# Top-32 attention with two feed-forward blocks on one core: mask into SBUF, short v matmuls, fixed scale for p, new instruction order

## The chip, the cores and the metric

The kernel runs on one core of a Trainium2 chip. The metric is the device time of one execution in microseconds, the median of several runs. One run more was recorded by the hardware profiler, and its trace is what the rows below come from.

## What is computed

```python
def _attn_ref(q, k, v):                       # (4, 8, 576, 64) each, float32
    scores = scale * np.matmul(q, k.transpose(0, 1, 3, 2))
    kth = np.partition(scores, -top_k, axis=-1)[..., -top_k:-top_k + 1]   # top_k = 32
    scores = np.where(scores >= kth, scores, -1000000000.0)
    attn = np.exp(scores - np.max(scores, axis=-1, keepdims=True))
    attn = attn / (np.sum(attn, axis=-1, keepdims=True) + 1e-09)
    return np.matmul(attn, v)
def _moe_ref(x, w_in, w_out):                 # x (2304, 512), w_in (512, 2048)
    h = x @ w_in
    return (h * (1.0 / (1.0 + np.exp(-1.702 * h)))) @ w_out
def _moe2_ref(x, w1, w2, w3, w_out):          # w1, w2 (512, 1024), w3 (1024, 1024)
    return (((x @ w1) * (x @ w2)) @ w3) @ w_out
```

The heads' outputs are put side by side as a (2304, 512) matrix, which goes through the first block and then through the second. The weights come as 64-bit floats.

## The kernel before, in words

**Tiles.** The 2304 rows are 18 tiles of 128. Each tile needs 8 heads of attention, so there are 144 heads, counted here from 0 (head 24 is the first of tile 3). Products are made in float16 with every operand split into a high and a low half: a block costs three matmuls, high by high, high by low and low by high (`product_op`, L780 to L782). A tile takes 168 such matmuls of 512 columns.

**A head** (`head`). Scores go into one of two PSUM score banks `s_ps` (L1084). VectorE takes the 32 largest by four maxima (L1106) and three replacements (L1109). ScalarE then masks in the bank itself (`f_cut`, L1124) and takes the exponential from the bank into SBUF (`f_exp`, L1127), after which the bank is free. The result is split into halves (L1133 or L1186, then L1136 and L1139), turned by a DMA transpose, and multiplied by v (`f_av`, L1154). For each head that is nine matmuls: five with the high half of the weights by 129 columns (64 of v's low half, 64 of its high half and one of ones), four with the low half by 65. ScalarE or VectorE copies the high part out (`f_x0`, L1209), and VectorE adds the low part (`f_x1`, L1213).

**A tile's blocks** (`moe`). Each operand is scaled by a row's mean of absolute values before it is split: x2 by L1360 and a reciprocal (L1377), p by one more ScalarE pass per half (`f_pa`, L1432), two VectorE steps (`f_psc`, L1438 and L1439) and the scaled split of `split_op` (L417, L420, L427, L430 to L440).

**Weights** (`weights`). 72 blocks of 512 KB are loaded, joined to 32-bit floats (L514), scaled by a norm (`l2_scale`) and split; w3's blocks are turned by four float32 matmuls with a scaled identity (`split_turned`, L677) and multiplied into w_out once (192 of the 512-column matmuls).

**Order.** All operations are recorded by `Order.op` and issued in the order of the table `PLAN`, which holds for each a rank and which of its alternatives (engine and form) is used. Each engine runs its own instructions strictly in that order, SP's DMA queue too.

Of the kernel before, what the change touches and what calls it, by code (L numbers as in the profile page):

```python
# [11 lines left out]
F32 = mybir.dt.float32  # L12
# [9 lines left out]
P = 128  # L22
# [15 lines left out]
class Order:  # L38
    GAP = {"T": 0.25, "V": 0.16, "A": 0.16, "G": 0.1, "D": 0.05, "N": 0.0}
    SAME = {"T": 0.0, "V": 0.11, "A": 0.12, "G": 0.1, "D": 0.25, "N": 0.0}  # L40
    DMA = 2.1
    COLD = ((100.0, 1.3), (300.0, 1.04))
# [33 lines left out]
    def run(self, log=None):  # L76
        free = dict.fromkeys("TVAGD", 0.0)
        lock = moved = 0.0
        for o in sorted(self.ops, key=lambda o: o.rank):
# [26 lines left out]
            if e == "D":  # L106
                moved = max(moved, now) + o.data
                o.end = max(o.end, moved) + o.lat
# [33 lines left out]
    'c-jq@1w$6i0)@9`Hl}uV_O;`sL_k8q4iH2@P(-l1yE{I+ySux)ySux)yIb%556?NzIkKcnNWv1AJW@U>zZB>#D1~@~y^3T=RAQ1X3CWfGq}<*--YBWKH'  # L142
    '%2NZX;L=HUkZ>4c*{$*rEyZYH^Lh!B}&z$no@gjGjBVoqf|?3BF&fLrA(=*)Kco;?du)t9pP;q+s!*jS}yIBc1gRvpS)jVE5v>Dnm*0s7Scp%x->&t=D'
    'jH0jOB6by_>wpq*u~=>4&8H`1ll(!(@NClYCb8lWWS`<sI@apCU>z-vPc;l*<Z`a(VN5qoop(D&_Fz^m?U2k|aUN^g2>@$ww;XEiILik|bX#)*I(7Csm'
    'RxDM%{pEh?3iLZvis6>n9khD4+=sfbioN|q9&dfw(zXKA!lL24^?m3m2IrOHxosgHM(G)<}~{pTI--5_n021v7{rP2ZEuryFwB5m>RmySsDq=V84?@8&'
    '5G*{Xu9rvD<&Pm&)``&*NkaNfvB*TZv+2s84UCHC)l>_9$@(t;?R8S6)qvZ!ul23|HhTK5DC;9pW%0Y6BoJTG#mzCq?Dl(N5<(59}<nD5clqzLNSyDBr'
    'j#OW2AT^X4NsXmeQX8p<)K6ODo#Q>^-5h&a+A6)4`b!HMENpP9LHF2^(hzBaG%R*z?2g!@v7MyF(n@KS)J2*sO_8Qbr(<7wUwHp`*GlW8OVSnTs&q}dF'
    '5QxDOAn>T(i7>a^h`P}Ka!uwPvvLwOZk=jS^gsbk^jp7WL=@k2kE<4mNhxMoJ;;D{gt5X_=L+*a#5cIxst5QIel`=!E$Z6sT?PllPk;VK5gW_@+hA%@>'
    'scv+)?f=_mc<7!{zdFnp{V&E033F$xGzrK5Kjy%B$qf@;09{@?&|0yjDIeACaHSFXW%Hq*zLJC5IBEgennAS*4&7tb{0~l?0`c(q8GN^igUmEtC#QSEa'
    'WyP${Y;DV3C3$`ECmvR>Jt>{L1`J(Y3FWM!GMO_`+3Q06L&l!MAe<&*MD`J*gU)+w8nW6DkCv9et`qMTE%DzBAqimXD_R7=S9d|LRlmfOn_az&r2J~ia'  # L150
    'Va;n_c=Rdi>JX+3@JNpclC&*Lfl5#D%gFIcHD-V=c%j<nM$UEiwa!;R;K6B)GavyoJ&tiF{yip!1uk+dKb4<P<&ye@~T$QiM59OKiQTe2NMZPH?l&|}|'
    '@p&hIl@G{o<?lYSVk!&dOFp;c*D_R&%fDpi>ngdG_i}!vu<uM|qoOLB0u+BGKq;h@P|7RSm9|RVa%&njX>_B}QRPaxC*|Ih8>*~rw4~9dM(xV2Xw;?A%'
    '0_3E3(7;~k@8mgs(e>|E4qqRTP>t|)v_vA^Q$@4a5bA6uLi5hYOeS&HApS4{#6v!Qkm+iIn+F=kLs^Rt08JBzbL;%zesh4T0&i;MyP3OIW<GA7T;B^uJ'
# [111 lines left out]
def kernel(  # L265
# [274 lines left out]
    def l2_scale(Es, turned=None, free=(), inv=None):  # L540
# [47 lines left out]
        if turned is None:  # L588
            return inv, sc, c
# [942 lines left out]
```

## Time and profile before

| what | value |
|---|---|
| median of three runs | 1005.24 us (1004.66 to 1005.38) |
| span of the profiled execution, first to last instruction | 1003.2 us |
| PE busy | 942.3 us, 94% |
| DVE busy | 916.6 us, 91% |
| ACT busy | 803.6 us, 80% |
| POOL busy | 811.5 us, 81% |

The profiled execution is told by its span; what lies around it makes the runs some 2 us longer. PE is TensorE's matmuls, DVE VectorE, ACT ScalarE, POOL GpSimd, SP the engine whose queue issues the DMAs. A busy time is the union of an engine's records, and records of consecutive instructions overlap: the pace of an engine is the distance from one start to the next.

### The profile page before, as it was taken

What the parts mean: (1) busy time and instruction counts of PE and PEld (TensorE: products, weight loads), DVE (VectorE), ACT (ScalarE), POOL (GpSimd) and SP (SyncE); (2) the same over time, 40 slices, a digit from 0 to 9 for tenths busy, and PEclk for the clock granted to TensorE, in tenths of its full rate; (3) what the DMA queues carried; (4) which work ended last, traced back from release to release, by engine and by line L of the source; (5) the groups of instructions that cost most, each with busy time, mean ns of one, the idle gap of its engine ahead of it and who ended that gap; (6) DMA issues with size and microseconds to landing.
All of it is one profiled execution on the core that took longest, in us unless ns stands there. A gap on an engine that the chain in (4) does not pass through costs nothing. (4 is left out here: it accounts for less than half of the span.)

```text
span 1003.2 us, 18918 instructions
## 1 busy us (share of the span) xinstructions
PE 942.3 (94%) x6011; PEld 497.7 (50%) x6011; DVE 916.6 (91%) x2012; ACT 803.6 (80%) x1519; POOL 811.5 (81%) x1199
## 2 busy tenths in 40 slices
PE   5688987899999989999999999999999999999998
PEld 3345553444545444555555555555455555554553
DVE  4899999999999999999999999999999999999543
ACT  7998999987878877998888987888797786756442
POOL 5977889988898999899989988989896886857212
PEclk7799998999999999999999999999999999999999
DMA  9999877977687676888777777767865967644301
GB/s 318 274 291 281 248 187 166 207 142 123 110 141 137 141 135 118 161 142 153 142 158 142 136 139 134 141 118 156 147 123 97 169 122 124 117 95 96 58 11 53
DMA packets 398564, 149.28 MB, mean 149 GB/s; under 512 B 376576, under 2 KB 384768, under 8 KB 398464
## 3 DMA queue, kind: packets, MB, share of 16 engines
q1 hardware_dynamic: 398464, 148.07, 71.9%
q8 instruction: 47, 0.77, 0.3%
q14 instruction: 53, 0.43, 0.2%
HBM read 52.43 MB, written 4.72 MB: 57 GB/s over the span
## 5 line engine op out<-in xcount | busy, mean ns | idle before, releaser
L1106 DVE MAX8 m8s<-ysb 128x8 f32<-128x576 f32 x432 | 322.6, 754 | 5.1
L1109 DVE MATCH_REPLACE8 ysb<-m8s,ysb 128x576 f32<-128x576 f32 x288 | 214.0, 743 | 0.0
L1139 POOL TENSOR_TENSOR ysb<-ysb 128x512 f16<-128x512 f32 x143 | 165.3, 1159 | 2.9 <-ACT ysb L1133 2.2
L1124 ACT ACTIVATE s_ps<-s_ps,m8s 128x576 f32<-128x576 f32 x144 | 102.4, 711 | 53.7 <-DVE m8s L1106 52.9
L780 PE MATMUL mm<-w,usb 128*128 128x512 f16 x350 | 133.1, 380 | 1.5 <-DMA usb<-usb 1.5
L782 PE MATMUL mm<-w,usb 128*128 128x512 f16 x350 | 132.9, 380 | 0.0
L781 PE MATMUL mm<-w,usb 128*128 128x512 f16 x350 | 132.9, 380 | 0.0
L782 PEld LDWEIGHTS <-usb 128*128 128x128 f16 x828 | 81.1, 98 | 98.6 <-issue 1.3
L1127 ACT ACTIVATE ysb<-s_ps,nbs,asm 128x576 f32<-128x576 f32 x144 | 119.7, 831 | 10.7 <-POOL nbs L1116 2.9
L780 PEld LDWEIGHTS <-usb 128*128 128x128 f16 x828 | 81.1, 98 | 90.3 <-issue 5.3
L781 PEld LDWEIGHTS <-usb 128*128 128x128 f16 x828 | 81.2, 98 | 83.9 <-issue 3.9
L1106 DVE MAX8 m8s<-s_ps 128x8 f32<-128x576 f32 x144 | 108.9, 756 | 9.8 <-PE s_ps L1084 7.7
L1084 PE MATMUL s_ps<-kts,qts 128*128 128x288 f16 (+1 forms) x640 | 96.9, 290 | 14.4 <-ACT ysb L1127 13.2
L780 PE MATMUL mm<-wout,usb 128*128 128x512 f16 x279 | 106.3, 381 | 2.2 <-DVE win L514 1.3
L1109 DVE MATCH_REPLACE8 ysb<-m8s,s_ps 128x576 f32<-128x576 f32 x144 | 107.7, 748 | 0.0
L782 PE MATMUL mm<-wout,usb 128*128 128x512 f16 x279 | 106.2, 381 | 0.0
L781 PE MATMUL mm<-wout,usb 128*128 128x512 f16 x279 | 106.2, 381 | 0.0
L1084 PEld LDWEIGHTS <-qts 128*128 128x128 f16 (+1 forms) x640 | 56.1, 101 | 59.5 <-issue 30.1
L1320 POOL TENSOR_TENSOR usb<-usb 128x512 f32<-128x512 f32 x57 | 72.4, 1272 | 12.4 <-issue 7.9
L1154 PEld LDWEIGHTS <-ats 128*128 128x128 f16 (+1 forms) x1440 | 73.8, 101 | 15.5 <-issue 4.2
L1154 PE MATMUL mm<-v2s,ats 128*128 128x129 f16 (+3 forms) x1440 | 77.2, 210 | 0.5 <-DMA ats<-ysb 0.3
L780 PE MATMUL mm<-win,usb 128*128 128x512 f16 x199 | 75.8, 381 | 0.4 <-DMA usb<-tsb 0.4
(374 smaller groups left out, 2235.8 us busy)
## 6 DMA issues: line engine op xcount, KB each, us to landing
w<-in_moe_w_out_dram SPq DMA_DIRECT2D x24, 512.0 KB, 5.5
w<-in_moe_w_dram SPq DMA_DIRECT2D x22, 512.0 KB, 5.8
w<-in_moe_w_in_dram SPq DMA_DIRECT2D x16, 512.0 KB, 5.6
qts<-qts SPq DMA_DIRECT2D x34, 128.0 KB, 2.4
out_dram<-usb SPq DMA_DIRECT2D x17, 256.0 KB, 2.4
usb<-in_q_dram SPq DMA_DIRECT2D x15, 256.0 KB, 3.5
usb<-in_k_dram SPq DMA_DIRECT2D x12, 256.0 KB, 3.0
usb<-in_v_dram SPq DMA_DIRECT2D x11, 256.0 KB, 3.1
```

Of the source, the lines that this page charges most:

```text
L780: nc.tensor.matmul(o, a[:, i, :], hi, start=(first and i == 0), stop=False)
L781: nc.tensor.matmul(o, a[:, i, :], lo, start=False, stop=False)
L782: nc.tensor.matmul(o, a[:, 4 + i, :], hi, start=False, stop=(last and i == 3))
L1084: nc.tensor.matmul(E["sp"][r : r + n, i], qe[q_][:, h, r : r + n], kt[:, j, i * HS : (i + 1) * HS], start=k_ == 0, stop=k_ == 1,)
L1106: nc.vector.max(out=E["m8"][:, 8 * i : 8 * i + 8], in_=E["sp"] if i == 0 else E["w"])
L1109: nc.vector.match_replace(out=two(E["w"]) if i == 0 else E["w"], in_to_replace=E["m8"][:, 8 * i : 8 * i + 8], in_values=E["sp"] if i == 0 ...
L1124: nc.scalar.activation(E["sp"], E["sp"], AF.Prelu, bias=E["m8"][:, TOPK - 1 : TOPK], scale=-1.0, alpha=1.0 / FAR)
L1127: nc.scalar.activation(two(E["y"]), E["sp"], AF.Exp, bias=E["nb"], scale=nesc)
L1139: return lambda: eng.tensor_tensor(hl()[:, S + SR : 2 * S], E["y"][:, 0:SM], hl()[:, 0:SM], op=ALU.subtract)
L1154: nc.tensor.matmul(heads_av()[r : r + n, j_, c0 : P + 1], e["at"][:, i, r : r + n], v2[:, j_, blk, c0 : P + 1], start=(i == 0), stop=(i == 8),
L1320: nc.gpsimd.tensor_tensor(E["f"], E["f"], E["f2"], op=ALU.mult)
```

## The change

What it does:

- The mask writes to an SBUF buffer of the pool `y`, and the exponential works in place there; the score bank is given back after the mask.
- In `f_av` all nine matmuls of a head take 65 columns (v's high half and the ones), and the five of the high half are each followed by one of 64 columns with v's low half into the same columns; each loads its weights anew. `f_x1` is gone.
- p is no longer measured: its scale is one constant, worked out once from the weights' norms (`q12`, `f_pinv`); p is split by `hi_lo`, without a scale.
- x2's scale comes from a sum of squares and the exponent bits of that sum, two small VectorE steps in place of a reciprocal.
- A w3 block may be turned by four transposes instead of four matmuls; the scale is then applied in the two copies.
- The scale factors of scores take two POOL steps instead of three; k's norm carries the 1/8.
- `PLAN` is new for all operations, and the planner's costs differ a little.

```diff
-    COLD = ((100.0, 1.3), (300.0, 1.04))
+    COLD = ((50.0, 1.28), (100.0, 1.03))
...
 PLAN = (
...
     def split_turned(W, scaled, E):
...
+        def f_in_t():
+            E["by"] = by
+            for i in range(4):
+                nc.tensor.transpose(bank()[:, i], W["w"][:, i * P : (i + 1) * P], ident)
...
+        def f_lo_t():
+            nc.vector.scalar_tensor_tensor(E["t"][:, 4:8], bank(), by, E["t"][:, 0:4], op0=ALU.mult, op1=ALU.subtract)
...
+        def f_both():
+            nc.vector.tensor_tensor(q12[:, 0:2], q12[:, 0:2], q12[:, 2:4], op=ALU.mult)
+
+        def f_across():
+            nc.tensor.matmul(M["mm"][0:2, 0:P], q12[:, 0:2], ident, start=True, stop=True)
+
+        def f_most():
+            nc.vector.tensor_reduce(most[0:2], M["mm"][0:2, 0:P], axis=mybir.AxisListType.X, op=ALU.max)
+
+        def f_all():
+            nc.tensor.matmul(M["mm"][:, 0:1], ones[0:2], upper(most)[0:2], start=True, stop=True)
...
-                    nc.gpsimd.tensor_scalar(e, kv_, sm[i, 1:2], D ** -0.5, op0=ALU.mult, op1=ALU.mult)
-
-                    nc.gpsimd.tensor_scalar(e, e, 2.0 ** -40, 2.0 ** 44, op0=ALU.max, op1=ALU.min)
-                    nc.gpsimd.tensor_scalar(sm[i, 8 + h0 : 8 + h1], e, -FAR, 1.0, op0=ALU.mult, op1=ALU.mult)
+                    nc.gpsimd.tensor_scalar(e, kv_, sm[i, 1:2], 2.0 ** 44, op0=ALU.mult, op1=ALU.min)
+                    nc.gpsimd.tensor_scalar(sm[i, 8 + h0 : 8 + h1], e, -FAR, -FAR * 2.0 ** -48, op0=ALU.mult, op1=ALU.add)
...
-            nc.scalar.activation(E["sp"], E["sp"], AF.Prelu, bias=E["m8"][:, TOPK - 1 : TOPK], scale=-1.0, alpha=1.0 / FAR)
+            nc.scalar.activation(two(E["y"]), E["sp"], AF.Prelu, bias=E["m8"][:, TOPK - 1 : TOPK], scale=-1.0, alpha=1.0 / FAR)
 
         def f_exp():
-            nc.scalar.activation(two(E["y"]), E["sp"], AF.Exp, bias=E["nb"], scale=nesc)
+            nc.scalar.activation(E["y"], E["y"], AF.Exp, bias=E["nb"], scale=nesc)
...
-                        c0 = 0 if i < 5 else D
+                        at_ = e["at"][:, i, r : r + n]
                         nc.tensor.matmul(
-                            heads_av()[r : r + n, j_, c0 : P + 1], e["at"][:, i, r : r + n], v2[:, j_, blk, c0 : P + 1],
-                            start=(i == 0), stop=(i == 8),
+                            heads_av()[r : r + n, j_, 0 : D + 1], at_, v2[:, j_, blk, D : P + 1], start=(i == 0), stop=(i == 8),
                         )
+                        if i < 5:
+                            nc.tensor.matmul(heads_av()[r : r + n, j_, 0:D], at_, v2[:, j_, blk, 0:D], start=False, stop=False)
...
-            def f_x1():
-                xs = X["x"][:, 2 * hp : 2 * hp + 2, 0:D]
-                nc.vector.tensor_tensor(xs, xs, heads_av()[:, :, 0:D], op=ALU.add)
...
-            nc.scalar.activation(x2e["h"][:, 0:C], x2e["mm"], AF.Abs, bias=tiny, scale=G13, accum_out=inv2)
+            nc.scalar.activation(x2e["h"][:, 0:C].bitcast(BF16), x2e["mm"], AF.Square, scale=2.0 ** 20, accum_out=inv2)
...
-            def f_pa(Ea=Ea, j=j):
-                nc.scalar.activation(Ea["f"], Ea["p"], AF.Abs, scale=G13, accum_out=pacc[j])
...
-            lo = split_op(
-                due, lambda E=E: E["h"][:, 0:C], lambda E=E: E["h"][:, C : 2 * C], lambda E=E: E["p"], psc, C, [c], E, ["p"],
-                acq=["h"], tag="p ", lo_dve=W,
-            )
+            lo = hi_lo(due, E, lambda E=E: E["p"], [pd[j]], ["p"], tag="p ")
```

What the new table makes of the order is shown at three places. The first is on PE, in the middle of one head's product with v: `ats` is the turned attention, `v2s` holds v's halves and `mm` is a PSUM bank. Before, from the last matmul of the high half on:

```order
L1154 LDWEIGHTS ats
L1154 MATMUL mm_96<-v2s,ats 128x129
L1154 LDWEIGHTS ats
L1154 MATMUL mm_96<-v2s,ats 128x65
L1154 LDWEIGHTS ats
```

And now, from the first matmul of a head on:

```order
L1195 LDWEIGHTS ats
L1195 MATMUL mm_96<-v2s,ats 128x65
L1199 LDWEIGHTS ats
L1199 MATMUL mm_96<-v2s,ats 128x64
L1195 LDWEIGHTS ats
```

Five wide matmuls of a head have become five pairs of short ones, with twice the weight loads; the four short ones behind them stay.

The second place is on DVE, the last rows ahead of the first maximum of head 24 (the last row in each fence). `ysb` and `s_ps` hold scores, `m8s` maxima, `wsm` constants of the weights, `xsb` the attention's output. Before:

```order
L1109 MATCH_REPLACE ysb<-m8s,ysb 128x576
L1213 TENSOR_TENSOR xsb<-xsb,mm_96 128x2x64
L888 RECIPROCAL wsm<-wsm 128x1
L1106 MAX m8s<-ysb 128x8
L889 RECIPROCAL wsm<-wsm 128x1
L1109 MATCH_REPLACE ysb<-m8s,ysb 128x576
L1106 MAX m8s<-s_ps_93 128x8
```

Now:

```order
L1150 MATCH_REPLACE ysb<-m8s,s_ps_94 128x576
L892 TENSOR_TENSOR wsm<-wsm 128x2
L1147 MAX m8s<-ysb 128x8
L893 TENSOR_TENSOR wsm<-wsm 128x1
L1150 MATCH_REPLACE ysb<-m8s,ysb 128x576
L1147 MAX m8s<-s_ps_93 128x8
```

The addition L1213 has gone, and the small steps on the weights' constants, which are more than before, stand further back.

The third place is on ACT, at the mask of head 60. Before, mask and exponential:

```order
L1124 ACTIVATE s_ps_93<-s_ps_93,m8s 128x2x288
L1127 ACTIVATE ysb<-s_ps_93,nbs,asm 128x576
L1028 ACTIVATE usb,asm<-usb,nbs 128x512
L1133 CAST ysb<-ysb 128x576
L965 COPY kvinv<-mm_96 128x1
```

Now:

```order
L1165 ACTIVATE ysb<-s_ps_93,m8s 128x576
L1168 ACTIVATE ysb<-ysb,nbs,asm 128x576
L1313 CAST usb<-usb 128x512
L1168 ACTIVATE ysb<-ysb,nbs,asm 128x576
L1174 CAST ysb<-ysb 128x576
```

The mask is the only one of the two that reads the score bank now, so exponentials stand where their other inputs allow and hold no bank.

## Rows read from the trace of the kernel before

**Rows 1.** Stretches: length, busy us (instructions) by engine, PE clock share, DMA share, GB/s.
```profile
0.00:50.00 50.00, 28.51 (x167) 17.49 (x168) 33.30 (x82) 43.05 (x91) 35.93 (x65) 0.76 0.98 296
50.00:125.00 75.00, 64.10 (x400) 38.37 (x399) 72.32 (x148) 68.43 (x122) 59.36 (x92) 0.98 0.97 275
125.00:200.00 75.00, 62.60 (x458) 35.10 (x456) 72.92 (x175) 73.51 (x141) 70.26 (x104) 0.93 0.84 184
200.00:237.50 37.50, 35.01 (x200) 17.74 (x201) 37.02 (x89) 33.59 (x61) 31.92 (x50) 1.00 0.73 138
237.50:400.00 162.50, 154.74 (x1037) 80.15 (x1035) 157.02 (x347) 129.91 (x251) 145.25 (x224) 0.99 0.71 131
400.00:925.00 525.00, 523.58 (x3314) 271.87 (x3312) 507.84 (x1111) 428.23 (x808) 449.45 (x643) 1.00 0.73 134
925.00:1003.20 78.20, 73.72 (x444) 36.95 (x442) 36.16 (x66) 26.87 (x53) 19.35 (x27) 0.99 0.19 42
```
**Rows 2.** The stretch from head 24's first maximum to the end, same columns.
```profile
237.50:1003.20 765.70, 752.03 (x4791) 388.97 (x4788) 701.01 (x1522) 585.00 (x1110) 614.05 (x892) 1.00 0.67 124
```
**Rows 3.** DVE in order of time: start us, us, instruction.
```profile
237.51 0.76 DVE L1106 MAX8 m8s<-s_ps 128x8 f32<-128x576 f32 x1
...
604.29 0.28 DVE L1213 TENSOR_TENSOR xsb<-xsb,mm 128x128 f32<-128x128 f32 x1
604.49 0.75 DVE L1106 MAX8 m8s<-ysb 128x8 f32<-128x576 f32 x1
...
611.27 0.16 DVE L963 RECIPROCAL kvc<-mm 128x1 f32<-128x1 f32 x1
611.35 0.74 DVE L1106 MAX8 m8s<-ysb 128x8 f32<-128x576 f32 x1
...
992.09 0.69 DVE L729 CAST tsb<-mm 128x512 f16<-128x512 f32 x1 [0.44 <-PE mm L711]
992.70 0.74 DVE L427 SCALAR_TENSOR_TENSOR usb<-psb,msm,usb 128x512 f16<-128x512 f32 x1
```
**Rows 4.** Who waited for whom from 225 to 400 us: total us, times, longest.
```profile
PE s_ps L1084 <- ACT ysb L1127: 6.8, 7, 2.9
```
**Rows 5.** PE in order of time around one pair of heads' product with v.
```profile
608.56 0.98 PE L1154 MATMUL mm<-v2s,ats 128*128 128x129 f16 x18
609.38 0.17 PE L953 MATMUL mm<-kvc,ones 128*128 128x1 bf16 x1
```
**Rows 6.** The chain that ended last: one 512-column matmul; 8 of 128 columns.
```profile
788.36 0.22 PE mm L781
...
947.66 0.45 PE mm L711 x8
```
**Rows 7.** PE in order of time among the weights: float32 and 16-bit matmuls.
```profile
75.42 1.05 PE L677 MATMUL mm<-tsb,win 128*128 128x128 f32 x8
76.52 1.05 PE L677 MATMUL mm<-tsb,win 128*128 128x128 f32 x8
...
137.27 1.10 PE L611 MATMUL mm<-w,tsb 128*128 128x512 f32 x2
138.21 0.38 PE L612 MATMUL mm<-wout,ident 128*128 128x512 f16 x1
```
**Rows 8.** Groups by line and shape: busy us, mean ns of one, idle before.
```profile
L1127 ACT ACTIVATE ysb<-s_ps,nbs,asm 128x576 f32<-128x576 f32 x144 | 119.7, 831 | 10.7 <-POOL nbs L1116 2.9 <-DVE nbs L1116 2.0 <-ACT usb L1311 0.5
L1124 ACT ACTIVATE s_ps<-s_ps,m8s 128x576 f32<-128x576 f32 x144 | 102.4, 711 | 53.7 <-DVE m8s L1106 52.9
L1432 ACT ACTIVATE usb<-psb 128x512 f32<-128x512 f32 x34 | 21.2, 626 | 14.5 <-POOL psb L1418 8.8 <-DVE psb L1412 5.7
L417 ACT ACTIVATE usb<-psb,msm 128x512 f16<-128x512 f32 x21 | 14.7, 714 | 1.1 <-DVE msm L1439 1.1
L1282 POOL TENSOR_TENSOR usb<-usb 128x512 f16<-128x512 f32 x57 | 65.9, 1158 | 2.1 <-ACT usb L1276 1.8
L430 POOL TENSOR_SCALAR psb<-psb,msm 128x512 f32<-128x512 f32 x12 | 8.3, 690 | 1.0 <-ACT usb L417 0.9
```

More of the change, by code (lines that the diff above doesn't have):

```diff
@@ L106, in run @@
             if e == "D":
-                moved = max(moved, now) + o.data
+                moved = max(moved, now + 0.3) + o.data
                 o.end = max(o.end, moved) + o.lat
@@ L545, in l2_scale @@
         sc = wcol()
-        d, ss = sc, inv
+        d, ss = sc if cols is None else cols, inv
         prev = None
@@ L866, in weights @@
         c_in, rin, r12 = wcols(NG), wcols(NG), wcols(2)
-        imax, c_x2, c_out, top, top3 = wcol(), wcol(), wcol(), wcol(), wcol()
+        imax, c_x2, c_out, top, top3, most, pinv = wcol(), wcol(), wcol(), wcol(), wcol(), wcol(), wcol()
         g13 = [(g[0], g[2]) for g in g3]
@@ L897, in weights @@
         ready["c12"] = dve_chain(
-            0.0, f_12, deps=d12 + [d4, ready["rin"]] + [g[1] for g in g13] + ready["in12"], rel=[("f", {"z": tsb[:, 0, :]}, "z")], tag="c"
+            0.0, f_12, deps=d12 + [pmost, d4, ready["rin"]] + [g[1] for g in g13] + ready["in12"], rel=[("f", {"z": tsb[:, 0, :]}, "z")], tag="c"
         )
@@ L957, in kv_prep @@
             2.1 if is_v else 1.7, due - 6, f_load, env=E, acq=[stage, "rest"] + (["v2"] if is_v else ["h", "kr", "kt"]), tag="kv load",
-            data=1.2, after=last_of.get(("load", is_v)),
+            lat=3.05, data=0.55, after=last_of.get(("load", is_v)),
         )
@@ L962, in kv_prep, with f_inv, f_inv_v @@
         s = pe(0.15, due - 1000, f_sum, deps=[a], env=E, acq=[("mm", E, "sum")], tag="kv sum")
-        c = dve(0.12, due, lambda: nc.vector.reciprocal(sc, E["sum"][:, 0:1]), deps=[s], tag="kv scale")
+        c = dve(0.085, due, lambda: nc.vector.reciprocal(sc, E["sum"][:, 0:1]), deps=[s], tag="kv scale")
+        part = 1.0 if is_v else D ** -0.5
+        def f_inv():
+            nc.scalar.activation(inv, E["sum"][:, 0:1], AF.Copy, scale=part)
+        def f_inv_v():
+            nc.vector.tensor_scalar(inv, E["sum"][:, 0:1], part, None, op0=ALU.mult)
         kinv = op(
-            [("A", 0.2, lambda: nc.scalar.copy(inv, E["sum"][:, 0:1]), 0.0), ("V", 0.12, lambda: nc.vector.tensor_copy(inv, E["sum"][:, 0:1]), 0.0)],
+            [("A", 0.05, f_inv, 0.0), ("V", 0.065, f_inv_v, 0.0)],
             due, deps=[c], env=E, rel=[("mm", E, "sum")], tag="kv inv",
@@ L1293, in moe @@
         xinv = mo[:, 0:1]
[L1294 to L1297 removed]
+        inv2, sc2, sg, uo = [mo[:, 2 + i : 3 + i] for i in range(4)]
+        thsc = mo[:, 6:10]
+        ths = pool(0.23, due - 30, lambda: nc.gpsimd.tensor_scalar(thsc, c_in, xinv, 1.0, op0=ALU.mult, op1=ALU.mult), deps=xt + [ready["c_in"]], tag="thsc")
         gs = []
@@ L1368, in f_lo, with f_sc2 @@
             )
+        def f_sc2():
+            nc.vector.tensor_scalar(
+                sc2.bitcast(U32), inv2.bitcast(U32), -1.0, float(223 << 23), op0=ALU.mult, op1=ALU.add
+            )
         def f_t2():
```

388 lines of the change are left out of this document (198 added, 190 removed).

## The prediction

> **What bounds the kernel now.** I read the stretches first, because shares over the whole span hide that the bound changes hands. From 50 to 237.5 us DVE is busy for 182.3 of 187.5 us and PE for 161.7 [rows 1]: VectorE sets the pace. From 125 to 200 us two others are as full: ACT 73.5 and POOL 70.3 of 75 us. From 400 to 925 us PE is busy for 523.6 of 525 us: TensorE sets the pace, and a faster VectorE is worth nothing there. Between 237.5 and 400 us both are near the top (154.7 and 157.0 of 162.5). The first 50 us belong to neither: PE has 28.5 us at a granted clock of 0.76, a mixture of its two levels 1.2 and 2.4 GHz, and the DMA engines are full at 0.98.
>
> So I cut the span where the bound changes hands, at head 24's first maximum on DVE, at 237.51 us [rows 3]. Behind it PE has 752.0 us of work in 765.7 us [rows 2]; 13.7 us are idle. PE's last matmuls end at about 999.2 us, so some 4 us of the idle time are the copy and the store of the last output. Of the rest the largest part has one cause: from 225 to 400 us PE waited seven times, 6.8 us in all, with a score product for the exponential that still read the bank [rows 4].
>
> The time after is then: when head 24 is reached, by VectorE's queue; what PE has left to do behind it; and what is left of PE's idle time.
>
> **VectorE's queue ahead of head 24.** Counted in the built order, ahead of that maximum, by start-to-start distances:
> - ten additions `f_x1` are gone, 0.20 us each (604.29 to 604.49) [rows 3]: -2.0 us;
> - five 512-wide scalings out of a bank and two casts fewer, mostly w3's blocks, priced as the cast, 0.61 us (992.09 to 992.70) [rows 3]: -4.3 us. The seven transposed w3 blocks add a 512-wide step each, but ten other steps of a weight split have gone, so the count of those stays level;
> - two 256-wide split steps fewer, about 0.4 us each, being half a 512-wide one and a fixed part: -0.8 us;
> - six small steps more (the scale from squares, the constant for p), one wider copy more, 0.08 us each for the small (611.27 to 611.35) [rows 3]: +0.8 us.
> The sum is -6.3 us. Some 18 us go over the whole kernel, for there are 72 additions, but what lies behind head 24 buys little while PE is full.
>
> **PE's queue.** The 3216 matmuls of 512 columns stay, at 0.22 us [rows 6], but 330 of them now stand ahead of head 24 where 342 did: twelve, 2.6 us, move behind it. Among the weights seven w3 blocks lose four float32 matmuls (1.10 us a block) and one 16-bit matmul (0.22), and gain four transposes. No row shows such a transpose; between four 128-column 16-bit matmuls (0.23 us) and the four it replaces (1.10) I take 0.35, the near end, as a transpose multiplies nothing. Against that seven more splits use a float32 pass of 0.94 us plus 0.22 [rows 7], and ten simple ones of 0.22 have gone. In all 7 x (0.35 - 1.32) + 7 x 1.16 - 2.2 = -0.9 us, ahead of head 24, where PE is not the bound: I count nothing.
>
> The product with v changes form. A pair of heads takes 18 matmuls in 0.82 us (608.56 to 609.38) [rows 5]; eight 128-column matmuls take 0.45, 0.056 each [rows 6]. Ten of 129 columns are then 0.57, and the eight short ones have 0.25 left, 0.032 each; if they cost by columns alone, 0.0285. I take 0.030. Now 28 x 0.030 = 0.84, against the 0.82 of before. Over 80 such groups (72 pairs, eight of which are cut at a batch's end and issue everything twice) that is +1.6 us, between -1.7 (at 0.0285) and +5.3 (at 0.032) without rounding, and +1.3 of it behind head 24. PE's work behind head 24 grows by 2.6 + 1.3 = 3.9 us.
>
> Here a rule speaks against the change. The trace shows a weight load ahead of every matmul and 128-column pairs at 0.056 us each [rows 6]. The Trainium skill (TensorE: Matmul & The Clock Gate, section Back-to-back issue gap) says that in a real stream of LDWEIGHTS and MATMUL pairs at N=128 about 81 ns pass per matmul. By it a pair of heads would take 2.27 us and the kernel some 116 us more; the trace does not agree (56 ns), so the sum goes by the rows.
>
> **PE's idle time.** The bank is now given back by the mask, and the exponential (0.83 us [rows 8]) and whatever stands between the two hold it no longer. Seven waits averaged 0.97 us, one of 2.9 us [rows 4]; each gets shorter by at least the 0.83 us. I count -4 us; the ends are 0, if PE's next matmuls wait for something else, and -6.8 us.
>
> **What costs nothing, and under what cover.** ACT loses 36 passes `f_pa` of 0.63 us and some 77 scaled passes of 0.71, and gains 31 casts [rows 8], at most 0.71: some 55 us fewer of 803.6. The mask now goes from PSUM to SBUF and the exponential from SBUF to SBUF. No row has these forms with these functions; the bounds are the two old durations, 0.71 and 0.83 [rows 8], so the pair costs up to 0.12 us more or less per head, 17 us at most, under what ACT loses. The Trainium skill (ScalarE: Activation LUTs, section Step-by-step) holds that ScalarE writes PSUM faster than SBUF, which would make the mask dearer; it changes no sum here, as ACT is busy for 585.0 of 765.7 us from 237.5 us on [rows 2], but it counts from 125 to 200 us, in a rival below.
> POOL gains ten 512-wide subtractions (1.16) and 49 scalings (0.69 [rows 8]), 45 us at most, and loses some 60 small steps: of its 40 idle us ahead of head 24, 4.7 lie between 125 and 200 us [rows 1], but most of the new work stands earlier. SP's queue has the same number of DMAs, and the 64th of 72 weight loads stands behind the 11th transpose of attention in both orders.
> p's split no longer waits for both halves of p, and loses about 1 us of latency; PE has other tiles' work over it, up to the end: nothing.
>
> **The sum.** -6.3 + 3.9 - 4.0 = -6.4 us on the span of 1003.2, so 996.8 us. The median of the runs is 2.0 us above that span: **998.8 us**.
>
> **The rivals.**
> *The pace was never VectorE's alone* (same). ACT and POOL are as full as DVE from 125 to 200 us. If they gate head 24, the -6.3 does not come, +3.9 is matched by idle time that PE had there, and the shorter waits for a score bank give back a microsecond or two: 1004 us. For it: 73.5 of 75 us on ACT. Against: ACT has less to do, POOL room before 125 us.
> *Short matmuls are held by their weight loads* (slower). Place: the 28 in a row of every pair, where now at most four stand in a row; the four may live on a load made early under a wide matmul. Price: 2240 of them. The gain of 6.4 us is gone when each takes 0.033 instead of 0.030, and at 0.038, nearer to the group's present mean of 0.046, they add 18 us: 1017 us. For it: nothing shows a long row. Against: the eight left-over short ones came out at 0.032 although each second to fourth had only a short one to hide under.
> *The skill's 81 ns* is the far end of the same mechanism: 1113 us, one chance in a hundred, since the 56 ns contradict it.
> *Constants arrive late* (slower). The chain of small VectorE steps that ends in `r12`, for which the first scaled copy of a waits (L1400, before at 254 us), now has five further links and is finished two heads later, behind head 28 instead of 26. If PE has nothing else ready, it stands for some of these two heads, 5 us or more in all: 1004 to 1009 us. Against: the order puts other tiles' products there.
> *The start gets shorter as well* (faster). Only 5.9 us of VectorE work stands ahead of the first maximum, by the same prices, where 11.3 did, and 16.7 of DVE's first 50 us are idle [rows 1]. If heads start 5 us earlier and keep that, 994; with all of the score waits gone too, 988 us.
>
> **How the numbers follow.** Two runs of this kernel differ by up to 0.7 us, so 0.2%, 2 us, is about what can be told from no change. The forecast's case has 0.52 (991 to 1002), the shorter start 0.14, no change 0.14, the two slower ones 0.11 and 0.08, the rule's 0.01. Faster by over 0.2%: 0.66; within: 0.14; slower: 0.20. The range that leaves out the lowest of the short starts and the dear half of the short matmuls is 986 to 1010.
>
> **What would show it.** Right: head 24's first maximum near 231 us; no wait of a score product for an exponential behind 225 us; a pair's 28 matmuls within 0.81 to 0.90 us; PE full from about 390 us. Wrong: 28 matmuls in over 0.95 us; head 24 at 237 us with ACT or POOL without gaps before it; PE idle around 250 to 265 us while the first copy of a waits for `wsm`.

## The result and the profile after

The changed kernel takes 992.06 us (median of four runs, 990.51 to 994.35) against 1004.95 us for the kernel before (1004.41 to 1005.38): a ratio of 0.9872, 95% interval 0.9853 to 0.9891, or 12.9 us less. A second set of runs on another chip gave 990.73 against 1004.90 us, 0.9861 (0.9843 to 0.9878). The forecast was 6.4 us less. Its direction was right and the time lies in its range; half of the gain was not in the sum.

The profiled execution took 994.35 us, the longest of its four, with a span of 992.6 us. The stretches of the kernel after, with the columns of [rows 1]:

```profile
0.00:50.00 50.00, 30.05 (x173) 18.22 (x174) 39.38 (x91) 42.10 (x92) 38.57 (x67) 0.83 0.98 307
50.00:125.00 75.00, 66.51 (x469) 38.61 (x468) 72.86 (x158) 73.50 (x136) 69.44 (x101) 1.00 1.00 283
125.00:200.00 75.00, 64.52 (x471) 33.53 (x471) 69.04 (x165) 68.08 (x126) 68.39 (x98) 0.95 0.82 182
237.50:400.00 162.50, 159.86 (x1252) 83.81 (x1251) 158.68 (x345) 126.92 (x249) 151.46 (x223) 1.00 0.78 143
400.00:925.00 525.00, 521.53 (x3778) 270.83 (x3776) 503.25 (x1056) 366.34 (x672) 450.51 (x621) 1.00 0.71 130
```

DVE (the third pair of numbers) is busy for 39.4 of the first 50 us instead of 33.3, and the first maximum of head 0 comes at 15.98 us instead of 26.11. From 125 to 200 us, where it had 2.1 us of idle time, it now has 6.0: a part of the lead is lost there in this execution (in the second, below, it has 2.9). ACT is relieved everywhere behind 125 us. Head 24's first maximum and the last head's (head 143), in VectorE's order of time of the kernel after:

```profile
226.87 0.75 DVE L1147 MAX8 m8s<-s_ps 128x8 f32<-128x576 f32 x1
...
906.99 0.74 DVE L1147 MAX8 m8s<-s_ps 128x8 f32<-128x576 f32 x1
```

Cut at the two, first the kernel before (its last head is at 926.50), then the kernel after:

```profile
0.00:237.51 237.51, 190.23 (x1222) 108.70 (x1223) 215.57 (x492) 218.60 (x410) 197.48 (x308) 0.92 0.89 229
237.51:926.50 688.99, 679.81 (x4354) 352.58 (x4352) 666.31 (x1459) 558.89 (x1059) 595.91 (x867) 1.00 0.72 133
926.50:1003.20 76.70, 72.22 (x437) 36.38 (x436) 34.69 (x64) 26.11 (x51) 18.13 (x26) 0.99 0.19 43
```

```profile
0.00:226.87 226.87, 186.97 (x1288) 103.66 (x1289) 208.15 (x478) 209.04 (x400) 201.00 (x300) 0.95 0.90 237
226.87:906.99 680.12, 673.54 (x4994) 351.35 (x4993) 659.43 (x1401) 492.26 (x919) 602.75 (x850) 1.00 0.73 133
906.99:992.60 85.61, 81.67 (x511) 40.73 (x509) 34.14 (x63) 28.73 (x52) 28.79 (x31) 1.00 0.27 58
```

Up to head 24 the kernel after is 10.6 us shorter; from there to the last head 8.9 us shorter; behind the last head 8.9 us longer, because TensorE still has 81.7 us of work there instead of 72.2. From head 24 to the end the two are equal, 765.7 us.

A pair's product with v on PE and the waits of score products (215 to 400 us, against [rows 4]), kernel after:

```profile
403.58 0.19 PE L1195 MATMUL mm<-v2s,ats 128*128 128x65 f16 x1
...
404.42 0.65 PE L1127 MATMUL s_ps<-kts,qts 128*128 128x288 f16 x4
```

```profile
PE s_ps L1127 <- ACT ysb L1165: 1.0, 3, 0.5
```

The 28 short matmuls take 0.84 us, 0.030 each. ScalarE's pair, by groups:

```profile
L1165 ACT ACTIVATE ysb<-s_ps,m8s 128x576 f32<-128x576 f32 x144 | 106.7, 741 | 77.5 <-DVE m8s L1147 72.5
L1168 ACT ACTIVATE ysb<-ysb,nbs,asm 128x576 f32<-128x576 f32 x144 | 124.5, 867 | 17.0 <-DVE nbs L1157 8.5
```

The mask takes 741 ns instead of 711, the exponential 867 instead of 831 [rows 8]: 0.07 us more per head, 9.5 us of ScalarE's time, within the bound of 17.

### The profile page after: what moved, and what is told of

Same layout as the page of the kernel before. It is cut to its first block, busy times and chain, and to the rows that moved or that the text cites. A ratio compares the mean times of both kernels' runs of the same rounds, so it can differ in the third digit from the quotient of the medians.

```text
span 992.6 us, 20241 instructions
## 1 busy us (share of the span) xinstructions
PE 942.2 (95%) x6790; PEld 495.7 (50%) x6790; DVE 901.7 (91%) x1939; ACT 730.0 (74%) x1369; POOL 832.5 (84%) x1180
## 5 line engine op out<-in xcount | busy, mean ns | idle before, releaser
L1165 ACT ACTIVATE ysb<-s_ps,m8s 128x576 f32<-128x576 f32 x144 | 106.7, 741 | 77.5 <-DVE m8s L1147 72.5
L789 PE MATMUL mm<-w,usb 128*128 128x512 f16 x388 | 147.1, 379 | 1.2 <-POOL usb L1319 1.0
L791 PE MATMUL mm<-w,usb 128*128 128x512 f16 x388 | 147.0, 379 | 0.0
L790 PE MATMUL mm<-w,usb 128*128 128x512 f16 x388 | 147.0, 379 | 0.0
L791 PEld LDWEIGHTS <-usb 128*128 128x128 f16 x912 | 89.1, 98 | 107.8
L789 PEld LDWEIGHTS <-usb 128*128 128x128 f16 x912 | 89.0, 98 | 100.2 <-issue 7.0
L1168 ACT ACTIVATE ysb<-ysb,nbs,asm 128x576 f32<-128x576 f32 x144 | 124.5, 867 | 17.0 <-DVE nbs L1157 8.5
L790 PEld LDWEIGHTS <-usb 128*128 128x128 f16 x912 | 89.1, 98 | 91.3 <-issue 2.1
L789 PE MATMUL mm<-wout,usb 128*128 128x512 f16 x304 | 115.3, 379 | 1.7 <-DMA usb<-usb 0.6
L791 PE MATMUL mm<-wout,usb 128*128 128x512 f16 x304 | 115.2, 379 | 0.0
L790 PE MATMUL mm<-wout,usb 128*128 128x512 f16 x304 | 115.2, 379 | 0.0
L789 PE MATMUL mm<-win,usb 128*128 128x512 f16 x220 | 83.5, 379 | 0.6 <-DMA usb<-usb 0.6
L791 PE MATMUL mm<-win,usb 128*128 128x512 f16 x220 | 83.4, 379 | 0.0
L790 PE MATMUL mm<-win,usb 128*128 128x512 f16 x220 | 83.4, 379 | 0.0
L1195 PE MATMUL mm<-v2s,ats 128*128 128x65 f16 (+1 forms) x1440 | 79.1, 194 | 3.4 <-DMA ats<-ysb 2.7
```

The source lines that it names most:

```text
L789: nc.tensor.matmul(o, a[:, i, :], hi, start=(first and i == 0), stop=False)
L790: nc.tensor.matmul(o, a[:, i, :], lo, start=False, stop=False)
L791: nc.tensor.matmul(o, a[:, 4 + i, :], hi, start=False, stop=(last and i == 3))
L1165: nc.scalar.activation(two(E["y"]), E["sp"], AF.Prelu, bias=E["m8"][:, TOPK - 1 : TOPK], scale=-1.0, alpha=1.0 / FAR)
L1168: nc.scalar.activation(E["y"], E["y"], AF.Exp, bias=E["nb"], scale=nesc)
L1195: nc.tensor.matmul(heads_av()[r : r + n, j_, 0 : D + 1], at_, v2[:, j_, blk, D : P + 1], start=(i == 0), stop=(i == 8),)
```

## The experiments

Three stretches tell the runs apart: to head 24's first maximum, from there to the last head's, and behind it (us, of the profiled execution). Each ratio is to runs of the kernel before on the same chip. The stretches are of one execution each: changed, changed_again and late_heads have the same work between head 24 and the last head, and differ there by 1.9 us (678.3 to 680.2).

| kernel | median us | ratio to before (95%) | to head 24 | to the last head | behind |
|---|---|---|---|---|---|
| before | 1004.95 | 1 | 237.5 | 689.0 | 76.7 |
| changed | 992.06 | 0.9872 (0.9853 to 0.9891) | 226.9 | 680.1 | 85.6 |
| changed_again | 990.73 | 0.9861 (0.9843 to 0.9878) | 222.5 | 680.2 | 85.3 |
| code_old_order | 1010.56 | 1.0050 (1.0032 to 1.0068) | 243.9 | 690.1 | 76.4 |
| old_order_no_mask | 1009.62 | 1.0048 (1.0032 to 1.0063) | 238.9 | 691.0 | 76.3 |
| new_start_old_rest | 1005.95 | 0.9998 (0.9983 to 1.0012) | 239.2 | 691.1 | 76.2 |
| early_heads | 1010.79 | 1.0053 (1.0038 to 1.0069) | 243.0 | 688.0 | 76.7 |
| late_heads | 996.20 | 0.9903 (0.9890 to 0.9917) | 229.5 | 678.3 | 85.6 |
| wide_av_x1 | 1004.81 | 0.9999 (0.9984 to 1.0013) | 225.9 | 692.5 | 85.6 |
| w3_matmuls | 997.82 | 0.9930 (0.9919 to 0.9942) | 227.4 | 684.5 | 85.3 |
| p_abs_back | 1007.14 | 1.0019 (1.0010 to 1.0027) | 223.1 | 694.7 | 87.5 |
| more_act | 996.72 | 0.9913 (0.9899 to 0.9928) | 225.4 | 683.6 | 85.7 |
| more_dve | 1027.78 | 1.0225 (1.0210 to 1.0240) | 224.7 | 714.3 | 85.7 |
| new_more_max | 999.00 | 0.9928 (0.9909 to 0.9947) | 224.0 | 687.5 | 85.7 |
| old_more_max | 1014.94 | 1.0083 (1.0061 to 1.0105) | 241.0 | 697.7 | 75.9 |
| no_v_low | 988.20 | 0.9829 (0.9813 to 0.9845) | 225.0 | 677.8 | 84.5 |
| old_no_v_low | 997.08 | 0.9914 (0.9894 to 0.9935) | 238.0 | 680.1 | 75.4 |
| mask_in_bank | 1260.07 | 1.2523 (1.2505 to 1.2541) | 271.6 | 898.4 | 87.8 |
| v_to_act | 993.46 | 0.9878 (0.9862 to 0.9895) | 223.8 | 681.6 | 86.5 |
| x0_on_act | 994.20 | 0.9894 (0.9873 to 0.9916) | 222.7 | 684.3 | 85.9 |

**The same kernel again.** No edit.

> The changed kernel once more, as the base for the three beside it. 990.5 to 994.5 us. Where its granted clock in the first 200 us is higher than in the first profile (0.83 and 0.95), its span should be shorter than 992.6 us, by 1 to 3 us, and the heads up to 24 earlier than 226.87.

Its span was 988.0 us, and the two executions of one program differ by 4.4 us before head 24 (222.49) and by nothing behind it (765.5 us):

```profile
0.00:222.49 222.49, 184.15 (x1288) 102.37 (x1288) 207.79 (x477) 208.41 (x400) 200.31 (x300) 0.95 0.93 242
```

DVE's work there is the same (207.8 and 208.2 us); its idle time is 14.7 us instead of 18.7. The clock from 125 to 200 us was 0.98 instead of 0.95, in the first 50 us 0.83 in both. So the execution was shorter with a higher clock, as expected, but by 4.6 us instead of 1 to 3, and that the clock is the cause is not shown.

**The code without the order.**

```diff
 PLAN = (
-    (ranks and alternatives of the changed kernel)
+    (those of the kernel before, operation by operation)
```

> The changed code in the order and with the engine choices of the kernel before (operations are matched by name and number; those that are new stand right behind what they need, the w3 blocks are turned by matmuls as before). Theory A (the code takes work away, the new order starts the heads earlier; the two are worth about half each): 997 to 1001 us, head 0's first maximum near 26 us as before, head 24's near 233 us, and the waits of score products for the exponential gone or short. Theory B (the order alone is worth it, the code nothing): 1003 to 1006 us. Theory C (the code alone): 991 to 994 us.

1010.56 us: none of the three. Up to head 10 its heads stand where they stood before (120.34 and 120.80 us), then they fall 6.0 us behind, at one place. POOL's waits of code_old_order from 115 to 150 us:

```profile
POOL ysb L1231 <- DMA ats<-ysb: 4.1, 1, 4.1
```

The mask takes its buffer of the pool `y` earlier than the exponential did, and here a cast found none free. Taking out the mask's part tests it:

```diff
-            nc.scalar.activation(two(E["y"]), E["sp"], AF.Prelu, ...
+            nc.scalar.activation(E["sp"], E["sp"], AF.Prelu, ...
-            nc.scalar.activation(E["y"], E["y"], AF.Exp, ...
+            nc.scalar.activation(two(E["y"]), E["sp"], AF.Exp, ...
```

> As code_old_order (the changed code in the order of the kernel before), but with the mask written into the score bank and the bank given back by the exponential, as before. There, POOL waited once for 4.1 us for a free buffer of the pool y, which the mask now takes instead of the exponential, and heads 12 and later came 6 us later than in the kernel before. Theory A (that stall is the whole loss; all else that the code takes away is not on the path in the old order): head 12 at 141 us and head 24 at 236.5 to 238 us as before, 1003 to 1006 us. Theory D (the code's savings on VectorE count, as the forecast had them: ten additions and a few small steps, 2 to 3 us, ahead of head 24): head 24 at 234 to 235.5 us, 1000 to 1003 us. Rival (the stall is something else): still 1009 to 1012 us.

The stall is gone (head 12 at 141.10 us, before 141.39), and head 24 comes at 238.9 us: theory A for head 12, and against theory D for head 24. The time, 1009.62 us, lies in the range of neither. Seventy-two additions fewer on VectorE buy nothing in the old order; the rest of it is even 1 to 2 us slower in each of the first two stretches, and 4.8 us slower in all by its ratio. What causes these was not found.

**The start.** First the changed kernel with its first heads put late (VectorE's maxima, replacements and joins alone, in their order):

```diff
 DVE
-join join join join max join mr max max mr mr max join mr join max join join
+join join join join join join join join join max mr max max mr mr max mr max
```

> The changed kernel, with nine of VectorE's steps of the first heads (maxima and replacements that stood among the first nine joins of weights) put behind the ninth join, at about 26 us, where the kernel before began with them. Nothing else moves. Theory A (VectorE's idle time in the first 50 us, which the heads' steps now fill, is what the forecast missed): nine steps of 0.72 us, 6.5 us, come back as later heads up to head 24 and at the end: 996 to 999 us. Rival (what is won at the start is lost again between 125 and 200 us, where ACT and POOL are full): 991 to 994 us, as the changed kernel.

996.20 us, theory A. Head 0 is at 26.04 us, as in the kernel before, head 24 at 229.51:

```profile
0.00:50.00 50.00, 26.32 (x143) 14.83 (x144) 33.06 (x79) 35.60 (x80) 32.54 (x57) 1.00 0.89 270
0.00:229.51 229.51, 184.80 (x1287) 102.37 (x1288) 208.74 (x477) 208.79 (x400) 200.62 (x300) 1.00 0.90 234
```

VectorE has the work of the changed kernel up to head 24 (208.7 us), but 20.8 us of idle time, 16.9 of them in the first 50 us; the two executions of the changed kernel have 18.7 and 14.7, of which 10.6 and 10.8 in the first 50 us. By the ratios the early start is worth 0.31 to 0.42%, 3.1 to 4.2 us. (This execution's clock was 1.00 throughout and its span 993.5 us, the median of its runs 996.2; so the spans show less of it.)

Then the kernel before, with two heads put early:

```diff
 DVE
-join join join join join join join join max join mr join max
+join join join max join max join mr mr join max max join mr mr join max max mr mr max max
```

> The kernel before, with nothing changed but the place of heads 0 and 1: their score products stand right behind the turned k on TensorE, and their 14 maxima and replacements among the first joins of weights on VectorE. Theory A: head 0's first maximum comes at 16 to 18 us instead of 26.1, some 4 to 6 us of VectorE's idle time are filled, and that stays to the end: 999 to 1002 us. Rival (the start is limited by loads and joins, and the joins that now come later cost as much): 1004 to 1007 us.

1010.79 us, slower than before: theory A falls for this order. Head 0 came at 18.25 us, but head 2 only at 53.59 (before 48.66). The waits on VectorE from 0 to 240 us:

```profile
DVE wout L510 <- ACT mm L506: 5.6, 5, 2.7
DVE m8s L1102 <- PE s_ps L1080: 4.8, 5, 2.1
```

Moving the steps of two heads forward moved VectorE's idle time behind them: up to head 24 it is 26.9 us, before 21.9. The last one gives the old order the whole start of the new one, on all engines:

```diff
 PLAN = (
-    (all ranks of the kernel before)
+    (ranks of the changed kernel through head 8, then those of the kernel before)
```

> old_order_no_mask, with the new order and its engine choices up to about 110 us (the first 32 maxima, through head 8), and the old order for the rest; the first nine heads' masks go to SBUF as the new order needs it. Theory A (what the start wins is kept): heads 8 to 24 some 8 to 11 us earlier than in old_order_no_mask, 999 to 1003 us. Rival (the old order's own waits between 125 and 200 us take it back): head 24 at 236 to 239 us, 1007 to 1011 us.

Head 8 came 11.1 us earlier than in old_order_no_mask (95.36 against 106.52), head 10 at 122.15 against 120.89: all lost at the seam. One wait shows it, among PE's from 95 to 122 us:

```profile
PE s_ps L1130 <- ACT ysb L1170: 9.3, 1, 9.3
```

A score product of the new order stands ahead of work of the old. So this run settles nothing on whether the start's gain would be kept.

**Undoing parts in the new order.**

```diff
+            X["x1", hp] = dve(0.2, due - 40, f_x1, deps=[x0], ...
```

> The changed kernel and its order, with the product with v as before: 129 columns wide for v's high half, and the addition of the low half's columns on VectorE, behind the copy. Theory D (the forecast: ten additions of 0.20 us ahead of head 24 cost 2.0 us, TensorE behind it saves 1.3 us): 992 to 994.5 us. Theory A (VectorE is the pace only where the order leaves it no gaps; the additions wait for ScalarE's copy besides): 994 to 999 us, with waits of the additions for the copy in the profile. Rival (nothing, TensorE bounds all): 990.5 to 992 us.

1004.81 us: the whole gain gone, more than any theory had. Not ahead of head 24, where the forecast put it (225.9 us), but behind:

```profile
225.92:918.38 692.46, 673.50 (x4328) 349.79 (x4327) 668.61 (x1461) 492.56 (x920) 601.68 (x850) 1.00 0.71 131
```

12.3 us more than in the changed kernel, with the same PE work and 9.2 us more on DVE. A wait of PE for the bank that the addition still read is 4.6 us of it:

```profile
PE mm L791 <- DVE xsb L1256: 4.6, 4, 2.4
```

```diff
-                nc.tensor.transpose(bank()[:, i], W["w"][:, i * P : (i + 1) * P], ident)
+                    bank()[:, i], W["w"][:, i * P : (i + 1) * P], turned, start=i == 0, stop=False, ...
```

> The changed kernel and its order, with the seven w3 blocks that are turned by transposes turned by float32 matmuls again, and their low halves made by one more matmul and a plain scaling. Seven times (1.10 + 0.22 - 0.43) = 6.2 us more on TensorE, all between 40 and 95 us. Theory of the forecast (TensorE is not the bound there, so nothing): 991 to 994 us. Rival (TensorE stands ahead of the heads in the first 100 us): 994 to 998 us, heads up to 24 later by 2 to 6 us.

997.82 us, in the rival's range: 5.8 to 7.1 us more, against 6.2 us of work put back on TensorE. But that work is not shown to be the price. Heads 6 to 10 are 1.5 to 3.0 us late, and between head 24 and the last head, where the edit puts no work, 4.4 us are lost. The matmuls of 512 columns wait there 7.3 us for operands that a DMA brings, in the second execution of the changed kernel 1.9. Ahead of head 24 the matmuls put back wait for ScalarE's copies, 6.3 us in all, where that line's fewer matmuls waited 2.0. How the one leads to the other was not found.

```diff
+            act(0.63, due, f_pa, deps=[p_], env=Ez, acq=["f"], rel=["f"], tag="p abs")
```

> The changed kernel and its order, with 36 passes of absolute values over p on ScalarE back (their sums are not used), 0.63 us each, 22.7 us in all, nearly all behind head 24. Theory of the forecast (ScalarE has room under VectorE and TensorE): 991 to 993.5 us. Rival (what ScalarE lost is a part of what the forecast missed): 994 to 998 us.

1007.14 us, worse than the rival. Heads up to 24 are as early as ever (223.05). ACT waited for p at the head of its queue:

```profile
ACT usb L1485 <- POOL psb L1469: 38.4, 22, 3.8
```

```diff
+            if h % 4 == 1:
+                nc.scalar.activation(E["y"][:, 0:C], E["y"][:, 0:C], AF.Abs)
```

> The changed kernel, with one more pass over 512 columns on ScalarE (absolute values in place, which changes nothing) right behind every fourth exponential, 36 in all, 0.6 us each, 22 us; it never waits, as its input is ScalarE's own. Theory of the forecast (ScalarE has the room): 991 to 995 us. Rival (ScalarE's time itself is on the path, as the run with p's passes put back suggests): 1000 to 1008 us. If this stays near 993, it was the waiting of those passes for p at the head of ScalarE's queue that cost 15 us.

996.72 us, between the theory and the rival. As much ScalarE time without a wait for another engine costs 4.7 to 6.0 us, not 15: by this comparison two thirds of p_abs_back's price come from where its passes stand and what they wait for. But ScalarE's time isn't free.

```diff
-            nc.scalar.activation(two(E["y"]), E["sp"], AF.Prelu, ...
+            nc.scalar.activation(E["sp"], E["sp"], AF.Prelu, ...
```

> The changed kernel, with the mask written into the score bank and the bank given back by the exponential, as before; where a score product stood between a head's mask and its exponential it is put behind the exponential in the order. Theory A (the earlier release is worth the 4 us that the forecast counted): 995 to 998 us, and score products wait for the exponential again, 5 to 13 us in all. Rival (TensorE has other work over it): 991 to 994 us.

1260.07 us, against both theories:

```profile
PE s_ps L1127 <- ACT ysb L1168: 159.7, 81, 6.4
```

In the new order score products stand between a head's mask and its exponential; put right behind the exponential they have no work of TensorE's to cover the wait. This prices that order without the early release, not the release.

**Which engine sets the pace behind head 24.**

```diff
+                    nc.vector.tensor_tensor(w2, w2, w2, op=ALU.add)
```

> The changed kernel, with an addition of 128 columns on VectorE, 0.20 us, behind the last maximum of every second head (72 in all); it works on a buffer that is free there, and nothing waits for its result. It is the time of the removed additions without their waits. Theory of the forecast (VectorE sets the pace up to head 24, TensorE behind): twelve of them ahead of head 24, 2.4 us: 993.5 to 996 us. Rival 1 (in this order VectorE's time counts everywhere, as the undone product with v suggests): 14 us, 1003 to 1007 us. Rival 2 (not its time but the bank that the old addition held was the price there): 991 to 993.5 us.

1027.78 us, beyond all three. The added steps did not take 0.20 us, so this run prices nothing. Their group, and that of the maxima of the run behind it:

```profile
L1221 DVE TENSOR_TENSOR ysb<-ysb 128x128 f32<-128x128 f32 x72 | 44.3, 616 | 2.5
```

```profile
L1221 DVE MAX8 spare<-ysb 128x8 f32<-128x128 f32 x72 | 19.8, 275 | 0.0
```

```diff
+                    nc.vector.max(out=spare, in_=E["w"][:, 0 : 2 * D])
```

> The changed kernel, with one more maximum over 128 columns on VectorE behind the last maximum of every second head (72 in all, some 0.2 us each, 14 us); its result is not used, it reads a buffer that is VectorE's own, and it shares nothing with POOL. Theory E (in the new order VectorE sets the pace from the start to the last head): 60 of them between head 24 and the last head, 12 us there, 1003 to 1006 us in all. Theory of the forecast (TensorE sets the pace behind head 24): twelve ahead of head 24, 2.4 us: 992 to 995 us.

> The same 72 maxima in old_order_no_mask (the changed code without the mask's part, in the old order; 1009.6 us, 691 us from head 24 to the last head). Theory E (in the old order TensorE sets the pace behind head 24, so that taking away 72 additions there bought nothing and putting 72 maxima back costs little): 1009 to 1013 us, the stretch from head 24 to the last head 691 to 694 us. Rival (VectorE sets it in either order): 1022 to 1025 us, 703 us.

999.00 us and 1014.94 us, each between its two theories. In both orders the stretch to the last head grew by about 0.64 of VectorE's added work there: 7.3 us for 11.5 in the new (from 680.2, beside changed_again), 6.7 for 10.4 in the old (from 691.0). With the 2 us that executions differ by, 0.64 may be 0.45 to 0.85. The forecast's theory falls: VectorE's time counts behind head 24. Theory E has too much of it for the new order and too little for the old.

```diff
-                        if i < 5:
-                            nc.tensor.matmul(heads_av()[r : r + n, j_, 0:D], at_, v2[:, j_, blk, 0:D], start=False, stop=False)
```

> The changed kernel without the ten matmuls per pair of heads that take v's low half (800 of the 2240 short ones; that part of the product is left out). 0.030 us each, 24 us in all, some 20 us of it behind head 24. Theory of the forecast (TensorE alone sets the pace behind head 24): 970 to 975 us. Rival (VectorE, busy for 694 of the last 766 us, or the order takes over): 978 to 988 us.

> old_order_no_mask without the ten matmuls per pair of heads with v's low half (that part of the product is left out), 16 us of TensorE's time between head 24 and the last head. In the new order the same cut shortened that stretch by 2.3 us. Theory E (TensorE sets the pace there in the old order): it falls from 691 to 677 to 682 us, 997 to 1001 us in all. Rival (neither engine alone, but the waits between them): 686 to 690 us, 1005 to 1008 us.

988.20 us, at the upper end of the rival's range, and 997.08 us, theory E. The stretches to the last head, first in the new order, then in the old:

```profile
225.03:902.84 677.81, 657.75 (x4325) 331.16 (x4324) 658.34 (x1401) 491.82 (x919) 601.66 (x850) 1.00 0.74 134
```

```profile
237.96:918.01 680.05, 664.79 (x4356) 333.75 (x4355) 659.51 (x1386) 529.81 (x986) 573.37 (x801) 1.00 0.73 135
```

Sixteen microseconds of TensorE's work fewer buy 2.4 us in the new order, little more than executions differ by, and 11.0 in the old (from 691.0). So TensorE's time counts there in the old order and hardly in the new, while added time of VectorE counts in both. That a saving of VectorE's earned nothing in the old order because TensorE's time counted too would fit, but is not shown.

**Can the prices be used?**

```diff
-alternatives: a copy x4 V, g hi x4 V, p hi x3 V, o x2 V
+alternatives: a copy x4 A, g hi x4 A, p hi x3 A, o x2 A
```

> The changed kernel, with 13 steps of 512 columns (four copies of a, seven casts of g and p, two copies of the output) made by ScalarE instead of VectorE, at the same places of the order. VectorE loses 4 x 0.60 + 7 x 0.37 + 2 x 0.61 = 6.2 us, ScalarE gains 7.0 us. By the prices of the runs before (0.55 and 0.25 for a microsecond) 3.4 less 1.75 us: 989 to 990.5 us. Rival (prices found by adding work don't hold for taking it away; the moved steps wait at the head of ScalarE's queue): 992 to 997 us.

```diff
-alternatives: x0 x15 V
+alternatives: x0 x15 A
```

> The changed kernel, with the 15 copies of a pair's product that VectorE makes (0.20 us each, 3 us) made by ScalarE (0.16 us each) at the same places. By the prices 1.6 less 0.6 us: 990 to 991 us, hardly to be told from the changed kernel. Rival (ScalarE waits for the product at the head of its queue): 992 to 996 us.

993.46 and 994.20 us: both in the rivals' ranges, and by the ratios 0.6 to 3.3 us more than the two measurements of the changed kernel, which is not clear of the intervals. So neither shows a gain. But v_to_act is no test of the price, as its stretch behind the last head shows:

```profile
905.41:991.90 86.49, 81.94 (x512) 40.75 (x510) 26.75 (x51) 35.95 (x64) 28.65 (x31) 1.00 0.27 57
```

VectorE has 51 instructions there instead of 63: twelve of the thirteen moved steps stand where no price was measured. In x0_on_act twelve of the fifteen stand between head 24 and the last head, but the gain by the prices is below what executions differ by. Whether time taken off VectorE pays is left open. The changed kernel stays the fastest that computes all of it.

## Why the prediction was half right

- **VectorE's queue ahead of head 24: -6.3 forecast, -10.6 measured** (-15.0 in the second execution). This is the step that failed. It counted work taken off, and put the change of VectorE's idle time at nothing without a reason. The work fell by 7.4 us (215.57 to 208.15; 7.8 in the second), near the forecast; the idle time fell as well, from 21.9 to 18.7 us, and to 14.7 in the second. The new order puts the first heads' maxima among the joins of weights, where VectorE had stood waiting. late_heads takes that back: VectorE's idle time rises again and 3.1 to 4.2 us are lost, half to two thirds of the 6.5 us that the sum missed. What the rest comes from is not shown. The prediction had this case among its rivals, *the start gets shorter as well*, with 994 us and a chance of 0.14. Its premise held: 6.4 us of VectorE's work stand ahead of the first maximum now, 12.1 before. The 16.7 idle microseconds [rows 1] on which it rested were in the first row read, and deserved more.
- **PE behind head 24: +3.9 forecast, +3.2 measured** (752.0 to 755.2). The product with v took 0.84 us a pair, 0.030 a matmul, as forecast, so the dear short matmuls are out. The rival made of the 81 ns that the Trainium skill (TensorE: Matmul & The Clock Gate, section Back-to-back issue gap) gives at N=128 is out with them: 128 columns took 56 ns [rows 6].
- **PE's idle time there: -4.0 forecast, -3.2 measured** (13.7 to 10.5). Score waits fell from 6.8 to 1.0 us. So this part of the sum, -0.1, came out at 0.0.
- **The reason given for that part was wrong, though its sum was right.** *A faster VectorE is worth nothing there* read PE's 523.6 of 525 us [rows 1] as the pace. That the heads behind 24 came 8.9 us faster, and this was given back behind the last head, where 9.4 us more of TensorE's work was left, would still fit it. The added maxima do not: a microsecond more on VectorE cost 0.64 in both orders, while one less on TensorE gave 0.7 in the old and 0.15, hardly to be told from nothing, in the new.
- **What costs nothing: not shown, and in doubt.** ScalarE's savings were put at nothing. In the new order 21 us more on it cost about 5 (more_act), and w3's matmuls in place of transposes about 6, where both were said to be covered. That these savings earned as much is not shown: in the old order all of the code's savings together earned nothing.
- **Against the median** 2 us more were missed: the sum was made on spans, and the profiled execution after was the longest of its four. In the second execution, 4.6 us shorter, the whole difference lies ahead of head 24, so these 2 us belong most likely to the step that failed.

The code alone makes nothing faster: in the old order it takes 1009.6 or 1010.6 us. The new order with only the product with v as before takes 1004.8. So the gain shown is that of work taken off together with an order that was fitted to it. All of the old code in the new order was not tried, so what the order is worth alone is open.

## What to carry to other kernels

When a change brings a new order, count the idle time of the engine that sets the pace as well as its work: what stands idle at the start is the first thing that a new order can fill, though moving the steps of two heads alone did not fill it (early_heads). A busy share of 99.7% doesn't say that an engine sets the pace; two engines can share it, and changing the work of one of them tells, if the changed steps stand in the stretch in question (in v_to_act they did not). And undoing one part at a fixed order prices the misfit along with the part, as mask_in_bank's 1260 us show: read such a run as an upper bound at best.

## What was not expected of the hardware

- The VectorE addition with both inputs in SBUF (more_dve) took between 291 and 2328 ns (median 486) for 128 columns; the addition with one input in PSUM took 234 to 290 ns in the kernel before, a maximum over as many columns 268 to 280. GpSimd was busy for 834.8 of the 1024.7 us of more_dve. The Trainium skill (GPSIMD Engine Reference, section 1. Specifications) says that GpSimd's way into SBUF is shared with VectorE and that instructions of VectorE with two SBUF inputs contend for it. By it only the first of the three would stretch, and the rows agree.
- Four transposes of a w3 block took 0.43 us (94.44 to 94.87), not the 0.35 that the forecast took between its bounds of 0.23 and 1.10:

```profile
94.44 0.60 PE L688 MATMUL mm<-ident,win 128*128 128x128 f32 x4
94.87 0.38 PE L837 MATMUL mm<-win,nid 128*128 128x512 f16 x1
```
